# Last layers: seven layer-1 blocks of unit 1 ahead of all layer 2, and the output weights' low parts and sums on VectorE

## The chip, the cores and the metric

One core of a Trainium2 chip runs the whole program. The metric is device time in microseconds (us), the median of several runs. The kernel before takes 671.37 us (three runs, 671.11 to 671.58).

Engines are named as in the profile: PE is TensorE, PEld its weight loads, DVE is VectorE, ACT is ScalarE, POOL is GpSimd, SP is SyncE, which issues most of the DMAs. Each runs its own instructions in program order and waits on semaphores for the others.

## The reference

Attention with pooled keys, then a mixture of eight experts of which each token uses one, then a last pair of dense layers in which the change lies:

```python
x = moe(attention(q, k, v))             # 2304 tokens x 512; tokens without a place in an expert are zero
h = x @ w_in                            # 512 x 2048, float64 weights
g = s * np.maximum(h, 0) ** 2 + b
out = (g @ w_out).astype(np.float32)    # 2048 x 512, float64 weights
```

`b` adds the same row to every token, `b` times the column sums of `w_out`.

## The kernel before

Every float32 product is made of three fp32r products (high x high, high x low, low x high), so each operand is split into a high part, a copy to fp32r, and a low part, the difference. The float64 weights come as pairs of int32 words and are first made into float32 by four steps on DVE per 128x512 piece (`Weights64.step`, L858, L861, L863, L867; here A, B, C, D) and an absolute value on ACT (L860) into one buffer `c_u`. At step B of a piece the piece before it is split: high part on ACT (L1371), low part on POOL (L1372).

The last layers (`last_layers`) work on units of 256 tokens. A unit has 16 blocks of 128 rows of the middle dimension. For one block layer 1 takes 12 matmuls into a PSUM bank (`layer1_y`, L1019); `square` makes relu on ACT (L1386) and its product with the bank on DVE (L1387) in one of four SBUF tiles `rt`; `parts` splits that into `gh` (ACT, L1392) and `gl` (POOL, L1393). Layer 2 takes six matmuls a block (L1398) into two banks that are kept for the unit, from `gh`, `gl` and the split piece `wo` of `w_out`.

`pair` does units 0 and 1 together while `w_out` is loaded (16 DMAs of 512 KB, L1433) and converted; 32 more DVE additions (`add`, L1419 and L1421) sum all high and low parts. The order is written out by hand: layer 1 of unit 0 (16 blocks, banks of all eight), layer 2 of its blocks 0 to 7, layer 1 of unit 1's blocks 0 to 7 (four banks, `ph`), layer 2 of these, layer 2 of unit 0's blocks 8 to 15, layer 1 of unit 1's blocks 8 to 15, their layer 2. Between these, `spare` puts one or two conversion steps into DVE's queue for each block. Unit 2 starts behind it; after its second block `rows` multiplies the sums by a matrix of ones (L1426).

Far ahead of this, in block 1 of the experts (`block(1)` in `main`), DVE also works through `tab`, a list of small steps that make a table of the remaining work: three steps at each of f = 3 to 7 of its layer 2, and three at each block of its layer 1.

Of the kernel before, what the change touches and what calls it, by code (L numbers as in the profile page):

```python
# [869 lines left out]


class Experts:
# [160 lines left out]
    def main(self, left, one, ps):  # L1033


        nc, tc, yt = self.nc, self.tc, self.yt
# [98 lines left out]
        def block(u, v=self.v):  # L1135
# [40 lines left out]
            for f in range(KF):  # L1176
# [4 lines left out]
                tab(u == 1, 3)  # L1181
# [164 lines left out]
def last_layers(nc, tc, c, a, pool, x, ps, out):  # L1346
# [15 lines left out]
    sums = {}  # L1362
    slots = raw[2:4]
# [10 lines left out]
    cv = Weights64(nc, KF2, lambda i: wo[i], split_out, lambda i: cf[i % 2], cu)  # L1374
    done = [0]

    def conv(n):
        for _ in range(n):
            if done[0] < cv.total:
                cv.step(done[0])  # L1380
                done[0] += 1

    def square(f, p, n):
# [3 lines left out]
        nc.vector.scalar_tensor_tensor(out=r, in0=p, scalar=0.0, in1=r, op0=ALU.max, op1=ALU.mult)  # L1387

    def parts(f, n=CU, at=None):

        at = f if at is None else at
        nc.scalar.copy(gh[:, at, :n], rt[f % 4][:, :n])  # L1392
        nc.gpsimd.tensor_sub(gl[:, at, :n], rt[f % 4][:, :n], gh[:, at, :n])  # L1393

    def layer2(p, j, f, c=slice(0, DM), at=None):
        at = f if at is None else at
        for i, (l, z) in enumerate(((gh, 0), (gh, 1), (gl, 0))):
            nc.tensor.matmul(p[:, c], lhsT=l[:, at, j * P:j * P + P], rhs=wo[f][:, z, c], start=f == 0 and i == 0, stop=f == KF2 - 1 and i == 2)  # L1398
# [17 lines left out]
    def add(i):  # L1416

        if i == 0:
            nc.vector.tensor_add(sums["acc"], wo[0][:, 0], wo[0][:, 1])  # L1419
        elif 1 < i < 2 * KF2:  # L1420
            nc.vector.tensor_add(sums["acc"], sums["acc"], wo[i // 2][:, i % 2])  # L1421

    def rows(p):
        acc, drop = sums["acc"], sums["drop"]

# [4 lines left out]
    def pair():  # L1430

        for i in range(KF2):
            nc.sync.dma_start(out=wo[i].rearrange("p c two -> p (c two)"), in_=wout[:, i])  # L1433
# [5 lines left out]
        adds = iter(range(2 * KF2))

        def spare(n):
            for _ in range(n):
                if done[0] < cv.total:
                    conv(1)
                    continue
                if "acc" not in sums:
                    nc.vector.memset(onesf, 1.0)
                    sums["acc"] = pool.tile([P, DM], F32, name="c_f0")
                    slots.append(pool.tile([P, DM], F32, name="c_f1"))
                    sums["drop"] = pool.tile([P, DM], F32, name="c_u0")  # L1450
                add(next(adds, 2 * KF2))
# [152 lines left out]
```

## Time and profile before

| | |
|---|---|
| median of three runs | 671.37 us |
| the profiled execution | 671.41 us, its span 669.4 us |
| PE busy | 598.1 us, 89% of the span |
| DVE busy | 390.7 us, 58% |
| POOL busy | 281.7 us, 42% |
| ACT busy | 254.5 us, 38% |
| mean granted PE clock | 0.942 of full speed |

The shares are means over a span whose stages have different limits. `pair` runs from 339 to 450 us; the table says nothing about that stage by itself. A row of the timeline is one instruction, or several alike: its start, how long, its engine, line and operation, and in brackets the idle time of its engine ahead of it and what ended that.

### The profile page before, as it was taken

The page shows a single profiled execution, that of the slowest core. Times are in us where ns is not written, and L with a number is a line of the kernel's source. Part 1 is how long each engine was busy: PE and PEld are TensorE (multiplying, and loading weights), DVE is VectorE, ACT ScalarE, POOL GpSimd, SP SyncE. Part 2 cuts the span into 40 slices and gives each one's busy share as a digit, 9 for nine tenths or more (in the row PEclk, how much of TensorE's full clock was granted, in tenths as well). Part 3 has the DMA queues.
Part 4 walks back from the last instruction along what each step waited for, and adds up shares of the span by engine and source line. Part 5 has one row for each costly group of instructions (what it writes and reads, how often), then busy time and mean ns, then how long its engine had stood idle before and what let it go on. Part 6 is the DMA issues. An engine that isn't in the chain of part 4 may idle for free.

```text
span 669.4 us, 11104 instructions
## 1 busy us (share of the span) xinstructions
PE 598.1 (89%) x4005; PEld 553.2 (83%) x4005; DVE 390.7 (58%) x876; ACT 254.5 (38%) x619; POOL 281.7 (42%) x306
## 2 busy tenths in 40 slices
PE   5797979689889979997997689899999999999896
PEld 5686878589889979996897488788889899898785
DVE  4599798976968958661629759993412022031140
ACT  1354455435535635533336334224314124043030
POOL 5458234414133506013219746453815326044291
PEclk8698799889979989997999789999999999999989
DMA  8988576536818994755549200017210100100000
GB/s 164 201 175 183 120 199 208 197 107 213 298 65 273 288 321 135 253 182 162 163 146 385 72 1 1 1 31 272 78 62 1 48 17 2 48 17 2 35 1 19
DMA packets 67949, 86.10 MB, mean 129 GB/s; under 512 B 24713, under 2 KB 40073, under 8 KB 67856
## 3 DMA queue, kind: packets, MB, share of 16 engines
q1 hardware_dynamic: 57696, 71.34, 35.2%
q10 hardware_dynamic: 7712, 6.84, 3.4%
q0 software_dynamic: 2448, 6.82, 3.2%
q8 instruction: 42, 0.69, 0.4%
q14 instruction: 51, 0.42, 0.2%
HBM read 68.09 MB, written 17.58 MB: 128 GB/s over the span
## 4 chain that ended last, share of the span: by engine, by line
PE 51%; DVE 24%; issue 9%; DMA 7%; POOL 5%; ACT 2%; SPq 1%; POOLq 0%; ACTq 0%; another core or an unknown queue 0%; DVEq 0%
PE bank L1398 10%; PE bank L1092 9%; PE bank L1019 7%; PE tq L1019 4%; PE misc L1019 4%; DVE c_f L1421 4%; DMA vraw<-in_v_dram 4%; PE bank L946 3%; PE bank L1227 2%; DVE c_f L863 2%; PE misc L946 2%; PE tq L946 2%; DVE c_f L861 1%; DMA wg<-in_moe_w_gate_dram 1%; DVE c_f L858 1%
## 5 line engine op out<-in xcount | busy, mean ns | idle before, releaser
L1398 PE MATMUL bank<-wo,gh 128*128 128x512 f32 (+1 forms) x448 | 134.6, 383 | 13.9 <-POOL wo L1372 9.6
L1393 POOL TENSOR_TENSOR gl<-rt,gh 128x256 fp32r<-128x256 f32 (+1 forms) x112 | 89.1, 804 | 78.4 <-ACT gh L1392 54.0
L1398 PEld LDWEIGHTS bank<-wo,gh 128*128 128x128 f32 x448 | 83.1, 192 | 32.5 <-POOL wo L1372 11.3
L1398 PE MATMUL bank<-wo,gl 128*128 128x512 f32 (+1 forms) x224 | 85.3, 381 | 0.0
L1092 PE MATMUL bank<-hs,w2h 128*128 128x288 f32 (+1 forms) x308 | 70.6, 318 | 4.9 <-issue 4.5
L915 POOL TENSOR_TENSOR w1l<-kraw,w1h 128x512 fp32r<-128x512 f32 x24 | 33.8, 1422 | 66.3 <-ACT w1h L911 66.2
L1405 DVE SCALAR_TENSOR_TENSOR raw<-bank,sb,c_u 128x512 f32<-128x512 f32 (+1 forms) x14 | 9.9, 710 | 85.5 <-PE bank L1398 85.5
L1092 PEld LDWEIGHTS bank<-hs,w2h 128*128 128x128 f32 x308 | 52.6, 199 | 5.8 <-issue 5.3
L1386 ACT ACTIVATE rt<-tq 128x256 f32<-128x256 f32 (+1 forms) x26 | 9.6, 368 | 116.9 <-PE tq L1019 93.4
L1398 PEld LDWEIGHTS bank<-wo,gl 128*128 128x128 f32 x224 | 43.1, 192 | 7.7
L1387 DVE SCALAR_TENSOR_TENSOR rt<-bank,rt 128x256 f32<-128x256 f32 (+1 forms) x60 | 24.2, 403 | 39.3 <-ACT rt L1386 39.3
L1092 PE MATMUL bank<-hs,w2l 128*128 128x288 f32 (+1 forms) x148 | 45.9, 310 | 0.0
L1392 ACT CAST gh<-rt 128x256 fp32r<-128x256 f32 (+1 forms) x112 | 43.2, 385 | 3.2 <-DVE rt L1387 3.0
L923 POOL DMA_INDIRECT xg<-xd,u_idx x23 | 26.0, 1130 | 34.9 <-DVE r L279 17.7
L1406 POOL DMA_INDIRECT out_dram<-raw,it x12 | 12.0, 999 | 62.6 <-DVE raw L1405 62.1
L1386 ACT ACTIVATE rt<-bank 128x256 f32<-128x256 f32 (+1 forms) x60 | 22.3, 371 | 40.8 <-PE bank L1019 27.0
L1372 POOL TENSOR_TENSOR wo<-c_f,wo 128x512 fp32r<-128x512 f32 x16 | 24.8, 1554 | 23.0 <-ACT wo L1371 23.0
L219 PE MATMUL sc<-kbd,qT 128*128 128x144 f32 (+1 forms) x152 | 26.3, 323 | 4.5 <-DVE rmine L369 2.8
L1092 PEld LDWEIGHTS bank<-hs,w2l 128*128 128x128 f32 x148 | 29.4, 198 | 0.0
L264 PE MATMUL o<-vx,eT 128*128 128x146 f32 (+1 forms) x144 | 24.3, 317 | 5.4 <-DVE lt L283 4.7
L219 PEld LDWEIGHTS sc<-kbd,qT 128*128 128x128 f32 (+1 forms) x152 | 22.7, 207 | 6.4 <-issue 3.5
L919 DVE TENSOR_TENSOR w2l<-vraw,w2h 128x512 fp32r<-128x512 f32 x39 | 26.8, 687 | 1.0 <-ACT w2h L918 0.5
(465 smaller groups left out, 1692.6 us busy)
## 6 DMA issues: line engine op xcount, KB each, us to landing
kraw<-in_moe_w_dram SPq DMA_DIRECT2D x14, 1024.0 KB
vraw<-in_moe_w_dram SPq DMA_DIRECT2D x14, 1024.0 KB
wo<-in_moe_w_out_dram SPq DMA_DIRECT2D x16, 512.0 KB
c_raw<-in_moe_w_in_dram ACTq DMA_DIRECT2D x13, 512.0 KB
kraw<-in_k_dram SPq DMA_DIRECT2D x8, 576.0 KB
out_dram<-c_u SPq DMA_DIRECT2D x1, 4608.0 KB
q<-in_q_dram SPq DMA_DIRECT2D x16, 256.0 KB
xd<-xr SPq DMA_DIRECT2D x16, 256.0 KB
```

The source lines that it names most:

```text
L219: nc.tensor.matmul(sc[:n, p // 2, p % 2 * 144:p % 2 * 144 + 144], lhsT=q[:, p, :n], rhs=kbd[b % 2][:, p], start=True, stop=True)
L915: eng.tensor_sub(self.w1l[:, i], self.w1(i), self.w1h[:, i])
L919: eng.tensor_sub(self.w2l[i], self.w2r[:, i], self.w2h[i])
L923: self.nc.gpsimd.indirect_dma_start(out=dst, out_offset=None, in_=self.xd[:have], in_offset=bass.IndirectOffsetOnAxis(ap=idx[:n], axis=0), ...
L946: self.nc.tensor.matmul(p, lhsT=l[:, f, k], rhs=r[k], start=n == 0, stop=n == 3 * KD - 1)
L1019: self.nc.tensor.matmul(p[:, :CU], lhsT=l[:, k], rhs=r[:, k], start=n == 0, stop=n == 3 * KD - 1)
L1092: nc.tensor.matmul(py[d][:, :v.n], lhsT=l[f][:, d * P:d * P + P], rhs=r[f], start=f == 0 and i == 0, stop=f == KF - 1 and i == 2)
L1386: nc.scalar.activation(r, p, AF.Relu)
L1392: nc.scalar.copy(gh[:, at, :n], rt[f % 4][:, :n])
L1393: nc.gpsimd.tensor_sub(gl[:, at, :n], rt[f % 4][:, :n], gh[:, at, :n])
L1398: nc.tensor.matmul(p[:, c], lhsT=l[:, at, j * P:j * P + P], rhs=wo[f][:, z, c], start=f == 0 and i == 0, stop=f == KF2 - 1 and i == 2)
L1421: nc.vector.tensor_add(sums["acc"], sums["acc"], wo[i // 2][:, i % 2])
```

## The change

In `pair`, the first seven blocks (`HEAD`) of unit 1's layer 1 now stand right behind unit 0's layer 1, ahead of all layer 2; then come layer 2 of blocks 0 to 6 of both units, layer 1 of unit 1's blocks 7 to 15, and layer 2 of blocks 7 to 15 of unit 0 and of unit 1. Parts of unit 1 lie in three spare tiles, in the places of the last two pieces of `w_out` (loaded later, behind layer 2 of the first seven blocks) and in places of `gh` and `gl` that unit 0 has left.

The low parts of `w_out` move from POOL to DVE (L1375), the split of unit 1's tokens too (`split_y`, at blocks 10 to 13 of unit 0). The 32 additions of high and low parts become 15 additions of whole pieces, in step C of the next piece, and a copy on ACT (L1380 and L1382). In every third block (f % 3 == 2) the product stays in the PSUM bank; ACT and DVE split it from there. In `block(1)` of the experts `tab` makes four steps at f = 2 to 7 of layer 2 and two at each block of layer 1.

```diff
 class Weights64:
-        self.pieces, self.total = pieces, 4 * pieces + 2
+        self.pieces, self.total = pieces, 4 * pieces + (3 if late else 2)
...
+        if s == 2 and self.late and 0 < i <= self.pieces:
+            self.late(i - 1, self.f(i - 1).bitcast(F32))
...
-                tab(u == 1 and f > 2 or u == 2, 3 if u == 1 or f < KF - 1 else 99)
+                tab(u == 1 and f > 1 or u == 2, 4 if u == 1 else 3 if f < KF - 1 else 99)
...
-                tab(u == 1, 3)
+                tab(u == 1, 2)
...
     def split_out(i, f):
         w = wo[i] = pool.tile([P, 2, DM], F32R, name=f"wo{i}")
         nc.scalar.copy(w[:, 0], f)
-        nc.gpsimd.tensor_sub(w[:, 1], f, w[:, 0])
+        nc.vector.tensor_sub(w[:, 1], f, w[:, 0])
+
+    def add(i, f):
+        if i:
+            nc.vector.tensor_add(raw[3], raw[3], f)
+        else:
+            nc.scalar.copy(raw[3], f)
...
-    def square(f, p, n):
+    def square(f, p, n, inside=False):
         r = rt[f % 4][:, :n]
         nc.scalar.activation(r, p, AF.Relu)
-        nc.vector.scalar_tensor_tensor(out=r, in0=p, scalar=0.0, in1=r, op0=ALU.max, op1=ALU.mult)
+        nc.vector.scalar_tensor_tensor(out=p if inside else r, in0=p, scalar=0.0, in1=r, op0=ALU.max, op1=ALU.mult)
...
+    def parts(f, n=CU, u=0, p=None):
+        h, l = place(f, u)
+        r = rt[f % 4][:, :n] if p is None else p
+        nc.scalar.copy(h[:, :n], r)
+        (nc.gpsimd if p is None else nc.vector).tensor_sub(l[:, :n], r, h[:, :n])
...
         def first(u, f0, f1, banks):
             for n, f in enumerate(range(f0, f1)):
                 p = banks[f % len(banks)][:, :CU]
                 if u or f >= EARLY:
                     x.layer1_y(u, p, *win[f])
-                square(f, p, CU)
-                spare(2 if u == 0 and n % 4 == 3 else 1)
+                inside = f % 3 == 2
+                square(f, p, CU, inside)
+                conv(1, steps_of_first)
+                if u == 0 and 10 <= f < 10 + KD:
+                    x.split_y(1, f - 10, nc.vector)
...
-        first(0, 0, KF2, ps)
-        for k in range(KD):
-            x.split_y(1, k, nc.gpsimd)
-        second(0, 0, KF, 2)
-        first(1, 0, KF, ph)
-        x.load_y(2)
-        second(1, 0, KF, 2)
-        second(0, KF, KF2, 2)
-        first(1, KF, KF2, ph)
-        tokens(2)
-        second(1, KF, KF2, 2)
-        for i in adds:
-            add(i)
+        first(0, 0, KF2, ps)
+        first(1, 0, HEAD, ph)
+        x.load_y(2)
+        second(0, 0, HEAD, steps_of_first)
+        second(1, 0, HEAD, steps_of_first)
+        for i in range(KF2 - 2, KF2):
+            wo[i] = pool.tile([P, DM, 2], I32, name=f"wo{i}")
+            load_out(i)
+        first(1, HEAD, KF2, ph)
+        conv(all_steps, steps_of_first)
+        second(0, HEAD, KF2, all_steps)
+        tokens(2)
+        second(1, HEAD, KF2, all_steps)
+        conv(all_steps)
```

`second` puts two steps (`conv(2, ...)`) behind each block's matmuls, as before.

On PE, the place behind unit 0's last block of layer 1 (`bank_1888`) read before:

```order
L1019 MATMUL bank_1888<-yhl,w2l 128x256
L1398 MATMUL bank_1885<-wo_16673,gh 128x512 x2
L1398 MATMUL bank_1885<-wo_16673,gl 128x512
L1398 MATMUL bank_1886<-wo_16673,gh 128x512 x2
L1398 MATMUL bank_1886<-wo_16673,gl 128x512
```

and reads now, with `y1h` and `y1l` the split tokens of unit 1:

```order
L1022 MATMUL bank_1888<-yhl,w2l 128x256
L1022 MATMUL tq<-y1h,w1h 128x256
L1022 MATMUL tq<-y1l,w1h 128x256
L1022 MATMUL tq<-y1h,w1l 128x256
L1022 MATMUL tq<-y1h,w1h 128x256
```

The first matmul that needs a piece of `w_out` stands 84 matmuls (seven blocks) later.

On DVE, one piece among the layer-2 blocks was four steps before (`c_f` the piece being made, two buffers in turn):

```order
L867 SCALAR_TENSOR_TENSOR c_f_16596<-c_u_16598,c_f_16596 128x512
L858 TENSOR_SCALAR c_f_16597<-wo_16609 128x512
L861 SCALAR_TENSOR_TENSOR c_f_16597<-wo_16609,c_f_16597 128x512
L863 SCALAR_TENSOR_TENSOR c_f_16597<-wo_16609,c_f_16597 128x512
L867 SCALAR_TENSOR_TENSOR c_f_16597<-c_u_16598,c_f_16597 128x512
```

and is six instructions now, with the low part of the piece before (`wo_17057`) behind B and its addition to the sum (`raw_1904`) behind C:

```order
L868 SCALAR_TENSOR_TENSOR c_f_16596<-c_u_16598,c_f_16596 128x512
L859 TENSOR_SCALAR c_f_16597<-wo_16609 128x512
L862 SCALAR_TENSOR_TENSOR c_f_16597<-wo_16609,c_f_16597 128x512
L1375 TENSOR_TENSOR wo_17057<-c_f_16596,wo_17057 128x512
L864 SCALAR_TENSOR_TENSOR c_f_16597<-wo_16609,c_f_16597 128x512
L1380 TENSOR_TENSOR raw_1904<-raw_1904,c_f_16596 128x512
L868 SCALAR_TENSOR_TENSOR c_f_16597<-c_u_16598,c_f_16597 128x512
```

The additions had stood in a row behind the last piece.

On DVE in unit 0's layer 1, blocks 9 to 12 now hold squares (L1400), steps, a low part in PSUM (L1415) and the split of unit 1's tokens (L1015):

```order
L862 SCALAR_TENSOR_TENSOR c_f_16596<-wo_16614,c_f_16596 128x512
L1375 TENSOR_TENSOR wo_16766<-c_f_16597,wo_16766 128x512
L1415 TENSOR_TENSOR gl<-tq,gh 128x256
L1400 SCALAR_TENSOR_TENSOR rt_1911<-bank_1883,rt_1911 128x256
L864 SCALAR_TENSOR_TENSOR c_f_16596<-wo_16614,c_f_16596 128x512
L1380 TENSOR_TENSOR raw_1904<-raw_1904,c_f_16597 128x512
L1015 TENSOR_TENSOR y1l<-yr,y1h 128x256
L1400 SCALAR_TENSOR_TENSOR bank_1884<-bank_1884,rt_1912 128x256
L868 SCALAR_TENSOR_TENSOR c_f_16596<-c_u_16598,c_f_16596 128x512
L1015 TENSOR_TENSOR y1l<-yr,y1h 128x256
```

Before, this place held squares and steps alone, and the tokens of unit 1 were split on POOL.

## Rows read from the trace of the kernel before

**Rows 1.** Stages of `pair`: window, length, busy per engine, clock, DMA share, GB/s.
```profile
339.16:362.18 23.02, 23.02 (x195) 22.82 (x193) 14.26 (x24) 10.36 (x30) 12.14 (x11) 1.00 0.74 266
362.18:390.37 28.19, 16.45 (x49) 11.36 (x49) 23.01 (x29) 11.69 (x27) 21.06 (x18) 0.81 0.35 131
414.06:427.77 13.71, 11.52 (x49) 8.86 (x48) 13.09 (x17) 3.62 (x7) 6.71 (x4) 1.00 0.00 0
438.82:449.74 10.92, 10.92 (x51) 9.02 (x49) 10.61 (x12) 2.31 (x7) 6.82 (x7) 1.00 0.16 48
```

**Rows 2.** Timeline of PE: waits in layer 2, and at `rows`.
```profile
378.84 0.80 PE L1398 MATMUL bank<-wo,gh 128*128 128x512 f32 x1 [5.03 <-POOL wo L1372]
...
453.90 1.12 PE L1426 MATMUL tq<-c_f,onesf 128*128 128x512 f32 x2 [1.17 <-DVE rt L1387]
```

**Rows 3.** Timeline of DVE at unit 0's layer 1, first piece and last square.
```profile
348.29 0.43 DVE L858 TENSOR_SCALAR c_f<-wo 128x512 int32<-128x512 int32 x1 [6.53 <-DMA wo<-in_moe_w_out_dram]
348.63 0.41 DVE L1387 SCALAR_TENSOR_TENSOR rt<-misc,rt 128x256 f32<-128x256 f32 x1
348.97 0.68 DVE L861 SCALAR_TENSOR_TENSOR c_f<-wo,c_f 128x512 int32<-128x512 int32 x1
...
369.11 0.43 DVE L1387 SCALAR_TENSOR_TENSOR rt<-bank,rt 128x256 f32<-128x256 f32 x1 [0.65 <-ACT rt L1386]
```

**Rows 4.** Timeline of DVE: one piece, POOL idle until its last D.
```profile
381.86 0.69 DVE L867 SCALAR_TENSOR_TENSOR c_f<-c_u,c_f 128x512 f32<-128x512 f32 x1
382.47 0.42 DVE L858 TENSOR_SCALAR c_f<-wo 128x512 int32<-128x512 int32 x1
382.92 0.69 DVE L861 SCALAR_TENSOR_TENSOR c_f<-wo,c_f 128x512 int32<-128x512 int32 x1
383.65 0.69 DVE L863 SCALAR_TENSOR_TENSOR c_f<-wo,c_f 128x512 int32<-128x512 int32 x1
384.44 1.56 DVE L867 SCALAR_TENSOR_TENSOR c_f<-c_u,c_f 128x512 f32<-128x512 f32 x1
```

**Rows 5.** Timeline of ACT and POOL at the same piece.
```profile
382.58 0.69 ACT L860 ACTIVATE c_u<-wo 128x512 f32<-128x512 f32 x1 [5.09 <-DVE c_f L867]
383.17 0.61 ACT L1371 CAST wo<-c_f 128x512 fp32r<-128x512 f32 x1
383.85 1.60 POOL L1372 TENSOR_TENSOR wo<-c_f,wo 128x512 fp32r<-128x512 f32 x1 [3.84 <-ACT wo L1371]
```

**Rows 6.** Timeline: DVE's additions beside POOL's `gl`.
```profile
434.46 0.84 POOL L1393 TENSOR_TENSOR gl<-rt,gh 128x256 fp32r<-128x256 f32 x1 [0.31 <-ACT gh L1392]
...
434.96 0.89 DVE L1421 TENSOR_TENSOR c_f<-c_f,wo 128x512 f32<-128x512 f32 x1
435.77 0.41 DVE L1387 SCALAR_TENSOR_TENSOR rt<-tq,rt 128x256 f32<-128x256 f32 x1
...
438.72 1.10 DVE L1421 TENSOR_TENSOR c_f<-c_f,wo 128x512 f32<-128x512 f32 x1
439.74 0.41 DVE L1387 SCALAR_TENSOR_TENSOR rt<-bank,rt 128x256 f32<-128x256 f32 x1
```

**Rows 7.** Instructions of L1012 on DVE: count, duration min/median/max in ns, first and last start.
```profile
L1012 DVE TENSOR_TENSOR yhl<-yr,yhl x4: 417/417/426, 336.7 to 337.7; 128x256 fp32r<-128x256 f32 x4
```

**Rows 8.** The chain that ended last: PE's first blocks behind a wait.
```profile
390.57 2.56 PE tq L1019 x12
...
393.13 1.65 PE misc L1019 x12
```

**Rows 9.** Experts' block 1 and 2: timeline of DVE and PE, and a window.
```profile
159.48 0.46 DVE L939 TENSOR_TENSOR xs<-tq,xs 128x288 fp32r<-128x288 f32 x1 [0.66 <-ACT xs L938]
...
185.33 0.45 DVE L949 SCALAR_TENSOR_TENSOR hs<-tq,hs 128x288 fp32r<-128x288 f32 x1
...
185.84 0.74 PE L937 MATMUL tq<-ident,xg 96*128 96x96 f32 x3 [3.36 <-DVE hs L949]
...
186.00:192.00 6.00, 6.00 (x27) 5.99 (x28) 3.00 (x10) 1.83 (x4) 1.74 (x1) 0.50 0.37 132
```

More of the change, by code (lines that the diff above doesn't have):

```diff
@@ L563 @@
 EARLY = 4
+HEAD = 7
 MORE = 64
@@ L1036, in main @@
         nc, tc, yt = self.nc, self.tc, self.yt
+        self.w = left
         w2h, w2l = self.w2h, self.w2l
@@ L1361, in last_layers @@
     ph, po = ps[0:4], ps[4:8]
-    sums = {}
-    slots = raw[2:4]
+    sums, more, spare, slots = {}, [], [], []
     v8 = lambda z: z.rearrange("p (k c) -> p k c", k=KD)
@@ L1375, in last_layers, with conv @@
+    steps = [(z, n) for z in cvs for n in range(z.total)]
     done = [0]
-    def conv(n):
+    def conv(n, end=len(steps)):
         for _ in range(n):
-            if done[0] < cv.total:
-                cv.step(done[0])
+            if done[0] < end:
+                z, i = steps[done[0]]
+                z.step(i)
                 done[0] += 1
-    def square(f, p, n):
+    def square(f, p, n, inside=False):
         r = rt[f % 4][:, :n]
         nc.scalar.activation(r, p, AF.Relu)
-        nc.vector.scalar_tensor_tensor(out=r, in0=p, scalar=0.0, in1=r, op0=ALU.max, op1=ALU.mult)
@@ L1389, in parts @@
[L1389 to L1398, printed above, removed]
+        nc.vector.scalar_tensor_tensor(out=p if inside else r, in0=p, scalar=0.0, in1=r, op0=ALU.max, op1=ALU.mult)
@@ L1400, in store, with layer2 @@
+    def layer2(p, j, f, c=slice(0, DM), u=0):
+        h, l = place(f, u)
+        for i, (g, z) in enumerate(((h, 0), (h, 1), (l, 0))):
+            nc.tensor.matmul(p[:, c], lhsT=g[:, j * P:j * P + P], rhs=wo[f][:, z, c], start=f == 0 and i == 0, stop=f == KF2 - 1 and i == 2)
     def store(u, j, p):
@@ L1414, in tokens, with load_out @@
                 x.split_y(u, k, nc.gpsimd)
[L1416 to L1421, printed above, removed]
     def rows(p):
-        acc, drop = sums["acc"], sums["drop"]
-        nc.tensor.matmul(p, lhsT=onesf, rhs=acc, start=True, stop=True)
+        drop = sums["drop"]
+        nc.tensor.matmul(p, lhsT=onesf, rhs=raw[3], start=True, stop=True)
         nc.vector.tensor_scalar(out=drop, in0=p, scalar1=sb[:, 1:2], scalar2=None, op0=ALU.mult)
         nc.sync.dma_start(out=out.rearrange("(n p) d -> p n d", p=P), in_=drop.unsqueeze(1).to_broadcast([P, T // P, DM]))
+    def load_out(i):
+        nc.sync.dma_start(out=wo[i].rearrange("p c two -> p (c two)"), in_=wout[:, i])
     def pair():
-        for i in range(KF2):
-            nc.sync.dma_start(out=wo[i].rearrange("p c two -> p (c two)"), in_=wout[:, i])
+        for i in range(KF2 - 2):
+            load_out(i)
             if i == 5:
@@ L1437, in pair @@
                     nc.sync.dma_start(out=sb[:, j:j + 1], in_=a[n].unsqueeze(0).to_broadcast([P, 1]))
+        more.extend(pool.tile([P, 2, 2, CU], F32R, name=f"wo{i}") for i in range(KF2 - 2, KF2))
+        spare.extend(x.w.tile([P, 2, CU], F32R, name=f"raw{i}") for i in range(3))
         held = []
[L1439 to L1451, printed above, removed]
+        nc.gpsimd.memset(onesf, 1.0)
         def first(u, f0, f1, banks):
```

26 lines of the change are left out of this document (19 added, 7 removed).

## The prediction

> **What bounds the kernel now.** I read the stages first, by windows, then PE's waits there, then the engine that these lead to. Layer 1 of unit 0 runs at full clock, 16 blocks in 23.02 us or 1.44 us each. Eight blocks of layer 2 at full clock take 10.92 us, 1.365 each, but the first eight take 28.19: PE is busy 16.45 of it, at a granted clock of 0.81, and unit 0's second eight take 13.71 [rows 1]. Against 10.92 that is 20 us over. PE's longest wait there is 5.03 us for a low part of `w_out` from POOL, and at `rows` it waits 1.17 us more for a square on DVE, which stands behind the last additions [rows 2]. Behind POOL stands DVE: it gets its first piece of `w_out` when the DMA lands at 348.29 [rows 3] and is busy 10.61 of 10.92 us still at the last eight blocks [rows 1]. So the stage is a queue of DVE work from 348.29 on, stretched by POOL; PE can gain at most what it waits for that queue.
>
> **The free pace of DVE.** With POOL idle, D to the next A is 0.61 us, A to B 0.45, B to C 0.73 [rows 4]; 0.61 is a 128x512 instruction followed by one that doesn't need its result. A followed by a square, or a square, takes 0.34 [rows 3]. A 128x256 subtraction from SBUF is 0.417 long [rows 7], as long as a square, which reads PSUM (0.41 long, 0.34 to the next [rows 3]); for it and for the one from PSUM, which no row shows, I take 0.36, between 0.34 and 0.42 if nothing overlaps: 0.7 us for all 11 below. Each of POOL's `gl` beside DVE makes an addition's start-to-next 0.81 to 1.02 [rows 6], so 0.20 to 0.41 more than 0.61; I take 0.31.
>
> **Stretch I: from 348.29 to the end of the seven blocks put ahead.** DVE has 22 squares x 0.34 = 7.5; 23 steps, of them 6 A x 0.34 = 2.0 and 17 B, C, D x 0.61 = 10.4; 5 low parts and 4 additions x 0.61 = 5.5; 7 low parts from PSUM and 4 of unit 1's tokens x 0.36 = 4.0. Sum 29.3. POOL keeps 15 `gl` beside them x 0.31 = 4.7. One wait for ACT of about the 0.65 seen at 369.11 [rows 3], taken as 0.5. DVE ends at 348.3 + 34.5 = 382.8. Check on the same engine before: from 348.29 to 369.11 [rows 3] stood 14 squares, 5 A and 13 other steps, 14.4 at the free pace, in 20.8 us, with POOL always busy. PE starts unit 1's block 0 piecemeal, as its tokens are split in blocks 10 to 13 of DVE's queue, and idles for some 6 us after 362; that is covered, since it waits for DVE later anyway.
>
> **Stretch II: layer 2 of the first seven blocks of both units.** DVE has 28 steps, seven pieces, without squares and with POOL idle. A piece's low part waits for ACT: D starts at 381.86, the absolute value behind it at 382.58, the copy at 383.17, and the subtraction that waited for the copy (on POOL then) started at 383.85, 1.99 after D [rows 4, 5]. On DVE alone it could start after 0.61 + 0.45 + 0.61 = 1.67, so 0.32 is a wait that the change adds; C, the addition and D stand behind it. Then three times 0.61 to the next D: 3.82 a piece, 26.7 in all (24.5 if the wait goes, at 3.5; with C to D at the 0.79 of a step that needs the one before it [rows 4] in three places, 4.4 a piece and 30.6). DVE ends at 409.5. PE meanwhile: piece 6's low part is done at 382.8 + 1.99 + 0.69 + 3.82 = 389.3, block 6 of unit 0 at 390.7, seven blocks of unit 1 at 400.2, four layer-1 blocks into the four banks at 406.0. Then it waits until DVE's square of block 7, 0.41 behind 409.5: about 410.0, a wait of 4 us.
>
> **Stretch III: the rest.** Behind a wait like that PE's first layer-1 blocks took 2.56 and 1.65 us at half clock [rows 8]. Block 11 ends at 412.6. Block 12 needs block 8's low part from PSUM: DVE has three squares, D, A, B, a low part and that one in front, 3.55 + 0.31 for a `gl`, so 413.4; it ends at 415.0, and three more x 1.44 at 419.4. Then 18 blocks of layer 2 x 1.365 = 24.6: unit 2 starts at 444.0. The last two pieces' loads follow 400 and their low parts end near 429, ahead of need; the sums too, so the wait of 1.17 at `rows` goes. Before, unit 2 started at 449.74 [rows 1]. Gain 5.7 + 1.2 = 6.9 us.
>
> **Experts' block 1.** The same steps of `tab` stand earlier. Before, PE waited 3.36 us for a read of a bank that DVE reached at 185.33, and then 6.0 us ran at a granted clock of 0.50, the lower of the two levels [rows 9]: 3.0 us lost. Now four steps more stand ahead of that read, about 0.7, but a first lot fills the 0.66 in which DVE waited at 159.48 [rows 9]. So that read stays where it was; the reads of blocks 0 to 5 come later, PE waits for these in pieces, and less at the end. Bounds: 3.3 gained (no drop of the clock) to 1.0 lost; I take 2.0 gained, nearer the row at half clock.
>
> **Sum.** 671.41, the profiled execution's own time (its span 669.4 and 2.0 around it; 0.04 above the median) less 6.9 and 2.0: 662.5, and I forecast 662.4 against the median. PE runs without a stage-sized wait from unit 2's start nearly to the end, so the shift stays.
>
> **Rivals.**
>
> *GpSimd's lock.* A `gl` of 0.84 us cost DVE 0.20 to 0.41 [rows 6]. If it costs its whole length in the thicker queue, where two of three DVE instructions read SBUF twice, stretch I grows by 15 x 0.53 = 8.0 and III by 0.5: 671.0, no change. For it: the D at 384.44 took 1.56 instead of 0.69 us beside POOL's `wo` [rows 4, 5]. Against it: the check above, where POOL was never idle, gave 20.8 for 14.4. The Trainium skill has this rule, on its page "SBUF — State Buffer", "Who interferes with whom": a Vector instruction with two SBUF inputs and a GpSimd instruction that reads SBUF block each other for the whole instruction. The additions' 0.20 to 0.41 show a part of it only.
>
> *The stretch isn't POOL's doing: slower.* If DVE's ratio of 20.8 to 14.4 comes from the mixture of squares and steps itself (waits for ACT among them), it holds in stretch I and II alike, though POOL has less to do: 29.3 + 24.5 (seven pieces at 3.5 free) times 1.45 is 78.0 where I have 61.2, and unit 2 starts 16.8 later: 679.2. It decides from 70.2 us on; between, each microsecond of the queue is one of the gain. For it: DVE's queue is longer than before at this point by low parts that were POOL's, and PE stands in order behind it. Against it: the free pieces at 381.86 to 383.65 [rows 4].
>
> *PE bounds it.* With no cost of `gl` and no wait for ACT, DVE needs 29.3 + 24.5, ends at 402.1, and PE waits only 2 us there; unit 2 starts near 436.0. With 3.3 from block 1: 653.2.
>
> **How the numbers follow.** Forecast 0.62; lock 0.13; slower 0.11; PE-bound 0.14. The forecast's own range is 658 to 668: 0.5 us on each of the seven pieces, 3 on stretch I, 2 on block 1. The range for 8 in 10 is 655 to 672; it leaves out the slower rival and the far end of the third. A measurement tells 0.2%, 1.3 us, from no change. Faster: 0.61 of the forecast's, 0.06 of the lock's and the third's 0.14, 0.81; within 0.2%: 0.08; slower 0.11.
>
> **What would show it.** Stretch I: DVE's seventh square of unit 1 near 381. Stretch II: D to D 3.8 us, with a wait for ACT of 0.3 ahead of each L1375. Stretch III: PE waits some 4 us near 406, then at L1022 half clock, and unit 2's layer 1 starts 5 to 6 us earlier against the experts' end than before. `rows`: no wait. Block 1: no window of 6 us at 0.50 behind 186. I am wrong if D to D is above 5.1 ((70.2 - 34.5) / 7), if PE doesn't wait for the squares behind the fourth block, or if the wait for banks at 186 is as long as before with the same clock.

## The result, and the profile after

The changed kernel took 665.51 us (median of 4 runs, 664.22 to 665.70) against 671.48 before (4 runs, 671.11 to 673.56): a ratio of 0.9901, 95% interval 0.9877 to 0.9924, which is 6.6 us less (the medians differ by 6.0). The forecast was 662.4, a ratio of 0.9866. The profiled execution took 665.48 and has a span of 663.8.

First, where the 5.6 us of span came from: PE's timeline at the places where stages begin and where it waits. Columns as in [rows 2].

```profile
157.17 0.51 PE L1096 MATMUL bank<-hs,w2h 128*128 128x288 f32 x2 [0.43 <-DVE u_lists L428]
...
215.65 0.43 PE L1096 MATMUL bank<-hs,w2h 128*128 128x288 f32 x2
...
410.05 0.38 PE L1022 MATMUL bank<-y1h,w2h 128*128 128x256 f32 x1 [3.81 <-DVE rt L1400]
...
413.52 0.58 PE L1022 MATMUL tq<-y1h,w2h 128*128 128x256 f32 x1 [1.24 <-DVE gl L1415]
...
445.62 0.41 PE L1022 MATMUL tq<-yhl,w1h 128*128 128x256 f32 x2
...
448.46 1.02 PE L1441 MATMUL tq<-raw,onesf 128*128 128x512 f32 x2
```

And the first two of these rows, block 1's and block 3's first product, in the kernel before:

```profile
153.17 0.51 PE L1092 MATMUL bank<-hs,w2h 128*128 128x288 f32 x2 [0.43 <-DVE u_lists L428]
...
214.36 0.43 PE L1092 MATMUL bank<-hs,w2h 128*128 128x288 f32 x2
```

The experts' block 1 starts 4.0 us *later* than before, behind instructions that are the same in both kernels. From there to block 3's first product (L1096; 215.65, 214.36 before) it is 58.48 for 61.19, 2.7 us gained. The first piece of `w_out` lands 0.96 later in the span (349.25 for 348.29). From the landing to `rows` it is 99.21 for 105.61 [rows 2, 3]: 6.4 us gained, `rows`' wait of 1.17 among them. Behind `rows` both take 210.7 to their last instruction. So the two edits gained 9.1 in this pair of profiles, and 4.0 went ahead of both.

The stages of `pair`, by windows (columns as in [rows 1]): layer 1 of unit 0; up to where layer 1 of unit 1 stood before; from block 8 of unit 1 into its block 12; the rest.

```profile
340.66:363.52 22.86, 22.86 (x196) 22.86 (x194) 14.69 (x30) 12.52 (x36) 7.66 (x9) 1.00 0.72 265
363.52:390.37 26.85, 22.04 (x127) 19.23 (x126) 25.85 (x49) 13.20 (x33) 7.95 (x8) 0.94 0.28 101
401.83:415.18 13.35, 8.30 (x57) 7.80 (x56) 12.79 (x25) 6.31 (x15) 2.48 (x3) 0.84 0.09 36
415.18:445.62 30.44, 30.44 (x150) 26.13 (x150) 12.86 (x22) 7.21 (x18) 6.81 (x8) 0.96 0.07 18
```

PE is busy 22.04 of 26.85 where it was busy 16.45 of 28.19 [rows 1], and the rest holds no wait. DVE is still full, 25.85 of 26.85 and 12.79 of 13.35. POOL has little to do.

DVE at the landing, at the end of stretch I (the sixth D, at 382.99), over one piece, and at the square of block 7:

```profile
349.25 0.43 DVE L859 TENSOR_SCALAR c_f<-wo 128x512 int32<-128x512 int32 x1 [5.99 <-DMA wo<-in_moe_w_out_dram]
...
382.99 0.68 DVE L868 SCALAR_TENSOR_TENSOR c_f<-c_u,c_f 128x512 f32<-128x512 f32 x1
383.59 0.41 DVE L859 TENSOR_SCALAR c_f<-wo 128x512 int32<-128x512 int32 x1
384.04 0.69 DVE L862 SCALAR_TENSOR_TENSOR c_f<-wo,c_f 128x512 int32<-128x512 int32 x1
384.96 0.69 DVE L1375 TENSOR_TENSOR wo<-c_f,wo 128x512 fp32r<-128x512 f32 x1 [0.23 <-ACT wo L1374]
385.57 0.68 DVE L864 SCALAR_TENSOR_TENSOR c_f<-wo,c_f 128x512 int32<-128x512 int32 x1
386.17 0.69 DVE L1380 TENSOR_TENSOR raw<-raw,c_f 128x512 f32<-128x512 f32 x1
386.77 0.68 DVE L868 SCALAR_TENSOR_TENSOR c_f<-c_u,c_f 128x512 f32<-128x512 f32 x1
...
409.58 0.42 DVE L1400 SCALAR_TENSOR_TENSOR rt<-bank,rt 128x256 f32<-128x256 f32 x1
```

A piece takes 3.78 from D to D, with the wait for ACT that the change adds (0.23) ahead of L1375.

At the end of the experts' block 1 PE waits in four pieces, and the 6 us behind the last of them run at full clock, where [rows 9] had one wait of 3.36 and a granted clock of 0.50 behind it:

```profile
178.99 0.54 PE L949 MATMUL bank<-xs,w1h 128*128 128x288 f32 x2 [0.81 <-DVE hs L952]
...
181.35 0.40 PE L949 MATMUL bank<-xs,w1h 128*128 128x288 f32 x1 [0.50 <-DVE hs L952]
...
185.39 0.54 PE L949 MATMUL misc<-xs,w1h 128*128 128x288 f32 x2 [0.47 <-DVE hs L952]
...
189.96 0.47 PE L940 MATMUL tq<-ident,xg 96*128 96x96 f32 x3 [1.13 <-DVE hs L952]
```

```profile
190.00:196.00 6.00, 6.00 (x49) 6.00 (x50) 3.52 (x8) 2.76 (x6) 2.12 (x2) 1.00 0.52 186
```

The four pieces still add up to 2.91 us. Most of the 2.7 gained there is therefore the clock, and only some 0.5 is waiting.

### The profile page after: what moved, and what is told of

The parts are those of the page before. It is cut to its first block, busy times and chain, and to the rows that moved or that the text cites. A ratio compares the mean times of both kernels' runs of the same rounds, so it can differ in the third digit from the quotient of the medians.

```text
span 663.8 us, 11041 instructions
## 1 busy us (share of the span) xinstructions
PE 596.7 (90%) x4005; PEld 554.0 (83%) x4005; DVE 377.2 (57%) x889; ACT 254.1 (38%) x620; POOL 241.9 (36%) x277
## 5 line engine op out<-in xcount | busy, mean ns | idle before, releaser
L1420 PE MATMUL bank<-wo,gh 128*128 128x512 f32 (+1 forms) x412 | 119.2, 374 | 1.2 <-ACT wo L1374 1.0
L1415 POOL TENSOR_TENSOR gl<-rt,gh 128x256 fp32r<-128x256 f32 (+1 forms) x96 | 72.6, 761 | 110.3 <-ACT gh L1414 59.2
L1420 PEld LDWEIGHTS bank<-wo,gh 128*128 128x128 f32 x412 | 74.9, 188 | 15.0 <-ACT wo L1374 1.4
L1420 PE MATMUL bank<-wo,gl 128*128 128x512 f32 (+1 forms) x206 | 76.8, 373 | 0.0
L1096 PE MATMUL bank<-hs,w2h 128*128 128x288 f32 (+1 forms) x308 | 69.1, 313 | 6.1 <-issue 5.7
L918 POOL TENSOR_TENSOR w1l<-kraw,w1h 128x512 fp32r<-128x512 f32 x24 | 34.0, 1432 | 64.8 <-ACT w1h L914 64.4
L1096 PEld LDWEIGHTS bank<-hs,w2h 128*128 128x128 f32 x308 | 51.3, 194 | 7.1 <-issue 6.5
L1096 PE MATMUL bank<-hs,w2l 128*128 128x288 f32 (+1 forms) x148 | 45.1, 305 | 0.0
L1420 PEld LDWEIGHTS bank<-wo,gl 128*128 128x128 f32 x206 | 38.8, 188 | 6.8
L1400 DVE SCALAR_TENSOR_TENSOR rt<-bank,rt 128x256 f32<-128x256 f32 (+1 forms) x53 | 21.3, 401 | 38.5 <-ACT rt L1399 38.2
L1414 ACT CAST gh<-rt 128x256 fp32r<-128x256 f32 (+1 forms) x96 | 36.6, 381 | 6.5 <-DVE rt L1400 6.5
L1400 DVE SCALAR_TENSOR_TENSOR rt<-tq,rt 128x256 f32<-128x256 f32 (+1 forms) x24 | 9.6, 400 | 36.4 <-ACT rt L1399 36.4
L1096 PEld LDWEIGHTS bank<-hs,w2l 128*128 128x128 f32 x148 | 28.7, 194 | 0.0
L264 PEld LDWEIGHTS o<-vx,eT 128*128 128x128 f32 (+1 forms) x144 | 20.2, 194 | 9.1 <-issue 7.1
L949 PE MATMUL bank<-xs,w1h 128*128 128x288 f32 (+1 forms) x120 | 26.1, 302 | 1.3 <-DVE hs L952 1.3
## 6 DMA issues: line engine op xcount, KB each, us to landing
wo<-in_moe_w_out_dram SPq DMA_DIRECT2D x16, 512.0 KB
c_raw<-in_moe_w_in_dram ACTq DMA_DIRECT2D x13, 512.0 KB
```

Of the source, the lines that this page charges most:

```text
L264: nc.tensor.matmul(o[:n, p // 2, p % 2 * 2 * VW:p % 2 * 2 * VW + 2 * VW], lhsT=et[:, p, :n], rhs=two_cols(vx[g][:, 2 * p:2 * p + 2]), star ...
L918: eng.tensor_sub(self.w1l[:, i], self.w1(i), self.w1h[:, i])
L949: self.nc.tensor.matmul(p, lhsT=l[:, f, k], rhs=r[k], start=n == 0, stop=n == 3 * KD - 1)
L1096: nc.tensor.matmul(py[d][:, :v.n], lhsT=l[f][:, d * P:d * P + P], rhs=r[f], start=f == 0 and i == 0, stop=f == KF - 1 and i == 2)
L1400: nc.vector.scalar_tensor_tensor(out=p if inside else r, in0=p, scalar=0.0, in1=r, op0=ALU.max, op1=ALU.mult)
L1414: nc.scalar.copy(h[:, :n], r)
```

## The experiments

The theory to be tested: each edit does what the prediction's steps say, and the 4.0 us ahead of them have nothing to do with the change. Beside the experiments the kernel before ran 44 times on three chips and took 667.34 to 676.16, so one time carries a chance of several us. Four lengths, one execution each, are therefore read from each trace as well: when block 1 starts; from there to block 3's first product ("blocks"); and, counted from the landing of `w_out`'s first piece, the square of block 7 (unit 1) and the start of unit 2.

```
kernel       block 1   blocks   square 7   unit 2   ratio to before (95%)
before       153.17    61.19      -        101.4    
before_2     157.58    59.90      -        102.2    (one time, 673.70)
before_3     155.50    61.01      -         99.9    (one time, 673.35)
tab_only     154.01    58.49      -        100.2    0.9968 (0.9943 to 0.9993)
pair_only    155.65    59.92    60.3        94.4    0.9892 (0.9854 to 0.9929)
after        157.17    58.48    60.3        96.4    0.9901 (0.9877 to 0.9924)
again        157.29    58.48    60.2        94.5    0.9902 (0.9867 to 0.9937)
low_on_pool  155.55    58.60    63.4        98.1    0.9857 (0.9819 to 0.9895)
no_inside    157.40    58.51    61.3        94.9    0.9835 (0.9801 to 0.9869)
order_only   152.87    58.48    64.5        98.7    0.9926 (0.9886 to 0.9965)
hold         159.56    58.47    53.2        95.7    0.9860 (0.9835 to 0.9885)
both         154.03    58.47    53.3        88.6    0.9783 (0.9757 to 0.9809)
all          157.20    58.46    51.5        86.9    0.9758 (0.9733 to 0.9783)
all_short    147.72    58.59    51.4        86.8    0.9646 (0.9600 to 0.9691)
```

**The two edits apart.** pair_only is the changed kernel with the old `tab` calls, tab_only the kernel before with the new ones:

```diff
-tab(u == 1 and f > 2 or u == 2, 3 if u == 1 or f < KF - 1 else 99)
+tab(u == 1 and f > 1 or u == 2, 4 if u == 1 else 3 if f < KF - 1 else 99)
...
-tab(u == 1, 3)
+tab(u == 1, 2)
```

> The change's last layers with the experts' tab steps back at their old places. The stages ahead of the experts' block 1 run the same instructions in every kernel here, and yet the changed kernel's block 1 started 4.0 us later than before (157.17 against 153.17). My theory: block 1's edit gained 3.5 us there (the later start of 4.0 us at 153 is down to 0.45 us at 217) and that is all it does. So here PE waits about 3.4 us in one piece near 190 and then runs at the lower clock for some 6 us, and the time is 665.5 + 3.5 = 669.0 if the 4.0 us come with the new last layers (another program behind the same early instructions). Rival: the 4.0 us come with the tab edit; then block 1 starts near 153 and the time is 665.0. Third: the early stages come out by chance in each program, anywhere from 1 us earlier to 5 us later than before; then the time less the start of block 1 is what carries the terms: 512.0 here against 508.3 after and 518.2 before.

> The kernel before with the tab edit alone. My theory: block 1 gains 3.5 us: no single wait of 3.4 us near 186, no 6 us at the lower clock behind it; time 671.4 - 3.5 = 667.9 with block 1 starting near 153. Rival, that the tab edit brings the late start: block 1 starts near 157, time 671.9. Third, that the start comes out by chance: the time less the start of block 1 is 514.7 wherever it starts (518.2 before).

With the old calls "blocks" is 59.90 to 61.19 in four profiles, with the new ones 58.46 to 58.60 in ten, whatever the last layers: 2.0 us on the means (60.5 and 58.5). pair_only shows the wait in one piece again:

```profile
188.34 0.74 PE L940 MATMUL tq<-ident,xg 96*128 96x96 f32 x3 [3.35 <-DVE hs L952]
```

```profile
188.50:194.50 6.00, 6.00 (x38) 6.00 (x39) 3.00 (x10) 2.21 (x6) 1.74 (x1) 0.73 0.42 127
```

The 6 us behind it run at 0.73 here and at 0.50 in the kernel before [rows 9]: 1.4 us of clock, where the two lengths differ by 1.3. In tab_only the longest such wait is 1.1. The ratios agree: 0.9968 is 2.2 us, 0.9892 is 7.3. They don't add up to the 6.6 us of both edits together; with intervals 3 to 5 us wide the times can't say why. pair_only came out at 665.71, not 669.0, and tab_only at 669.62, not 667.9: the expectation had read block 1's worth (3.5) and the 4.0 us from a single pair of profiles. Block 1 started at 155.65 and 154.01, neither 157 nor 153, as only the third reading (chance) allows; but the time less that start is 508.2 and 515.7 in the profiled executions (663.85 and 669.67), where that reading had 512.0 and 514.7: what follows varies by some us too.

**Where the 4.0 us come from.** again, before_2 and before_3 are the two kernels unaltered.

> The changed kernel unaltered, once more. The program before took 667.75 to 675.45 us in 17 runs beside the first experiments, and four profiles of kernels that run the same instructions up to the experts' block 1 started it anywhere from 153.2 to 157.4. My theory: the 4.0 us by which block 1 started later than before in the first profile were chance; the edits are worth 6.7 (last layers) and 2.1 (block 1) of the time before, a ratio of 0.987 to the kernel before on this chip. In the profile, counted from the landing of the first piece of w_out: the fifth multiplication that ends a piece (L868) ends stretch I at 33.7, the square of block 7 stands at 60.3, unit 2 starts at 94 to 97. Rival: the early stages are slower in this program for good: block 1 starts at 157 again and the ratio is 0.990 or more.

> The kernel before, unaltered, for its trace. My theory: the start of the experts' block 1 comes out by chance, by whether a short VectorE instruction with two inputs in SBUF (L149, L337) starts while a GpSimd addition of 1.3 to 2.4 us (L145, L147) runs; then it ends when that ends. Two paths were seen: L149 at 0.29 and the first L337 at 0.20 us, block 1 at 153.2 to 155.7; or both at 1.2 to 1.3, block 1 at 155.6 to 159.6. Both paths were seen with the new last layers, the second never yet in the two profiles with the old. By my theory this profile may show either. Rival: the second path belongs to programs with the new last layers; then here the first, block 1 at 153 to 154.

> As before_2, a third profile of the kernel before. By chance: either path, block 1 between 153 and 160. Rival: the first path again, 153 to 154.

again came out as its rival said, on both counts: block 1 at 157.29 and a ratio of 0.9902. But the kernel before starts block 1 at 153.17, 157.58 and 155.50 in three executions, against the rival that it always starts early: a late start isn't the new program's alone. A place where the ways part is near 44 us, in attention. DVE and then POOL there, in the kernel before as first profiled:

```profile
45.20 0.41 DVE L147 TENSOR_TENSOR vraw<-vraw 128x256 f32<-128x256 f32 x1
45.65 0.29 DVE L149 TENSOR_TENSOR vp<-vraw 128x128 f32<-128x128 f32 x1
...
45.93 2.36 POOL L145 TENSOR_TENSOR kraw<-kraw 72x1024 f32<-72x1024 f32 x1 [2.12 <-DMA kraw<-in_k_dram]
```

In the changed kernel:

```profile
44.09 2.35 POOL L145 TENSOR_TENSOR kraw<-kraw 72x1024 f32<-72x1024 f32 x1 [2.04 <-DVE lt L283]
46.52 1.32 POOL L147 TENSOR_TENSOR kraw<-kraw 72x512 f32<-72x512 f32 x1
...
44.17 2.56 DVE L147 TENSOR_TENSOR vraw<-vraw 128x256 f32<-128x256 f32 x1
46.76 1.23 DVE L149 TENSOR_TENSOR vp<-vraw 128x128 f32<-128x128 f32 x1
```

And in before_2, the late one of the old kernel:

```profile
44.80 2.32 DVE L149 TENSOR_TENSOR vp<-vraw 128x128 f32<-128x128 f32 x1
...
44.38 2.59 POOL L145 TENSOR_TENSOR kraw<-kraw 72x1024 f32<-72x1024 f32 x1 [1.41 <-DMA kraw<-in_k_dram]
```

POOL starts when what it waits for is there, a load in two of the three. If that is after DVE's two short instructions, they take 0.41 and 0.29; if POOL is 0.08 us ahead, as in the changed kernel, the first takes 2.56 and ends just behind POOL's (46.73, POOL 46.44), and the next waits for POOL's next. Later places of the same kind (L337, 0.20 or 1.30) follow. Over the 13 profiles (all_short apart) the two ways stay apart: seven with that L149 at 1.23 to 2.32 and a long first L337 (0.78 to 1.31) reach the last L337 at 142.7 to 145.2 us, the other six at 140.4 to 141.9.

That is part of the 4.0 alone. From the last L337 (141.08 before, 143.54 after, 2.5 later) to block 1 the two executions differ by another 1.5, with PE at another granted clock. The kernel before, then the changed one:

```profile
141.10:153.17 12.07, 11.02 (x88) 10.55 (x89) 9.68 (x54) 5.76 (x14) 0.23 (x1) 1.00 0.43 138
```

```profile
143.50:157.17 13.67, 12.55 (x89) 12.09 (x89) 10.07 (x55) 5.79 (x14) 0.23 (x1) 0.88 0.48 165
```

In all 13 this stretch takes 12.1 us at a granted clock of 1.00 (three profiles), 13.4 to 13.6 at 0.87 to 0.88 (five) or 14.3 to 14.7 at 0.78 to 0.80 (five), for old and new programs alike and on either way. So the 4.0 us are some 2.5 that go with the way taken near 44 us and some 1.5 of clock. All this is settled ahead of any instruction that the change touches.

What the runs don't settle is whether the new program falls into the late way more often. Of the four profiles with the old last layers one goes it, of the nine with the new ones six, and in these six L147 is held (1.66 to 2.56 us), which none of the old four shows. Block 1 started at 155.1 in the mean of the four, at 156.3 in the nine, and the ratio of again is 2.4 us short of the forecast's, at the edge of its interval.

**Where low parts are made.** low_on_pool puts `w_out`'s low parts on GpSimd again, no_inside all low parts of blocks, order_only both:

```diff
-        nc.vector.tensor_sub(w[:, 1], f, w[:, 0])
+        nc.gpsimd.tensor_sub(w[:, 1], f, w[:, 0])
...
-                inside = f % 3 == 2
+                inside = False
```

> The changed kernel with the low parts of w_out on GpSimd again, all else kept. My theory: on VectorE a low part costs 0.61 and a wait of 0.24 for ScalarE; on GpSimd it takes 1.6 and stretches one VectorE instruction by 0.87 (1.56 for 0.69 before), so a piece of stretch II stays at about 3.9 us (3.80 after), and PE gets piece 6 0.9 us later: 666.5, range 665 to 668. Rival, the lock for the whole instruction: each of 13 low parts ahead of the square of block 7 costs VectorE 1.6 - 0.85 more, 9.8 us: 675. Other rival, VectorE gains all 0.85 back in each piece: 13 x 0.85 = 11 us less queue, of which PE can use the 8 us that it loses near 410: 657.5.

> The changed kernel with every block's low part on GpSimd from SBUF, none on VectorE from PSUM. My theory: ahead of stretch II VectorE is spared 7 x 0.36 = 2.5 us and pays for 7 more instructions of GpSimd at 0.26 to 0.31 each, 2.0: no change, 665.0, range 664 to 666.5. Rival, the lock for the whole instruction (0.84 each): 7 x 0.84 - 2.5 = 3.4 us later: 668.9. Rival, GpSimd costs VectorE nothing in the mean: 663.0.

> The changed kernel's order, with both of its edits to low parts undone: GpSimd makes every low part of w_out and of each block, as before. Counted from the landing of the first piece of w_out: low parts of w_out on GpSimd alone moved the square of block 7 from 60.3 to 63.4, and all the blocks' low parts on GpSimd alone to 61.3. My theory: the two add up, square of block 7 at 64.4, unit 2 at 98 to 100 (94.4 to 96.4 in the changed kernel, 100.2 to 101.4 before, and before has a wait of 1.2 behind it too); the order alone is then worth some 3 us, less than half of the last layers' gain, and the ratio to before is 0.993 with block 1's 2 us. Rival: GpSimd now has the most to do (22 + 7 instructions), and its queue sets the end of stretch I: unit 2 at 101 or later, no gain from the order. Other rival: the order does it all, and moving work between the two engines nothing: unit 2 at 96 or less.

Square 7 answers, since it came at 60.2 to 60.3 in all three profiles of the changed last layers: 63.4, 61.3 and 64.5, expected 60.3 + 3.1 + 1.0 = 64.4 for the last. Expected for the first two were a delay of 0.9 us and none. Unit 2 comes at 98.7 in order_only, against 99.9 to 102.2 before with 1.2 more at `rows`. So the order, with the shorter sums and the tokens' split on VectorE that order_only keeps, is worth some 3.5 us and the low parts on VectorE some 3.5, of 7.2 in all; the two halves rest on one execution of order_only. By `rows` low_on_pool alone loses 3.0 (100.9 for 97.9) and no_inside nothing (97.7): the split in PSUM brings no gain that a run shows.

The times don't resolve the halves, and went another way than expected: low_on_pool took 663.26 (expected 665 to 668) and no_inside 661.93 (664 to 666.5). no_inside has the best ratio of the three and order_only (0.9926) the worst, with intervals some 5 us wide; that of no_inside ends at 0.9869, below the 0.9877 at which that of the changed kernel begins. Which stage makes no_inside faster isn't shown.

The last addition of one piece and the first rows of the next in low_on_pool, DVE and then POOL:

```profile
388.02 0.69 DVE L864 SCALAR_TENSOR_TENSOR c_f<-wo,c_f 128x512 int32<-128x512 int32 x1
388.63 1.75 DVE L1380 TENSOR_TENSOR raw<-raw,c_f 128x512 f32<-128x512 f32 x1
390.30 0.68 DVE L868 SCALAR_TENSOR_TENSOR c_f<-c_u,c_f 128x512 f32<-128x512 f32 x1
...
388.20 1.63 POOL L1375 TENSOR_TENSOR wo<-c_f,wo 128x512 fp32r<-128x512 f32 x1 [2.44 <-ACT wo L1374]
```

The instruction that was under way when POOL started keeps its 0.69; the one that starts 0.43 into POOL's 1.63 lasts until 0.55 behind POOL's end. So the price is about what is left of POOL's instruction when the next VectorE instruction comes: 1.06, with 1.20 left, and a piece takes 4.06 to 4.10 for 3.80. A `gl` in the changed kernel shows the same, POOL first:

```profile
354.52 0.92 POOL L1415 TENSOR_TENSOR gl<-rt,gh 128x256 fp32r<-128x256 f32 x1 [1.01 <-ACT gh L1414]
...
354.77 1.22 DVE L1375 TENSOR_TENSOR wo<-c_f,wo 128x512 fp32r<-128x512 f32 x1
```

It ends at 355.99, 0.55 behind POOL. An instruction that reads PSUM isn't held. Beside the next `gl` a square keeps its 0.41, and that `gl` takes 0.74:

```profile
356.84 0.74 POOL L1415 TENSOR_TENSOR gl<-rt,gh 128x256 fp32r<-128x256 f32 x1 [1.40 <-ACT gh L1414]
...
357.18 0.41 DVE L1400 SCALAR_TENSOR_TENSOR rt<-bank,rt 128x256 f32<-128x256 f32 x1
```

The Trainium skill's page "SBUF — State Buffer", "Who interferes with whom", says that a Vector instruction with two SBUF inputs and a GpSimd instruction that reads SBUF block each other for the whole instruction. The rows at 388.63 and 354.77 agree for a VectorE instruction that comes second.

**PE's wait for the square of block 7.** hold leaves 7 of stretch II's 28 steps for later (one step a block of unit 1 in place of two); both does so (three steps a block) and takes each block of layer 2 for unit 0 and unit 1 before the next block (`tokens(2)` then stands behind block 11); all adds an earlier split of unit 1's tokens, and has ScalarE make a piece's high part (early) ahead of the next piece's absolute value:

```diff
 hold
-        second(1, 0, HEAD, steps_of_first)
+        second(1, 0, HEAD, steps_of_first, 1)
 both
-        second(0, 0, HEAD, steps_of_first)
-        second(1, 0, HEAD, steps_of_first)
+        both(0, HEAD, steps_of_first, 3)
...
-        second(0, HEAD, KF2, all_steps)
-        second(1, HEAD, KF2, all_steps)
+        both(HEAD, KF2, all_steps, 4)
 all
-                if u == 0 and 10 <= f < 10 + KD:
+                if u == 0 and 8 <= f < 8 + KD:
...
+        if s == 1 and self.early and 0 < i <= self.pieces:
+            self.early(i - 1, self.f(i - 1).bitcast(F32))
```

> The changed kernel with 7 of the 28 conversion steps of stretch II left for later, so that VectorE's square of block 7 isn't queued behind them. My theory: the square of block 7 comes at 60.3 - 7 x 0.95 = 53.7 after the landing of w_out's first piece, PE's wait of 3.8 us there and the half clock behind it go, but pieces 13 to 15 end later and unit 0's blocks of layer 2 wait for them: unit 2 starts at 95 to 98 after the landing (94.4 and 96.4 in two profiles without the edit): no gain, 0 to +1.5 us. Rival: VectorE's later pieces are ahead of need anyway, PE keeps what it saves, some 7 us: unit 2 at 88.

> As hold, and in both parts of layer 2 each block is taken for unit 0 and unit 1 before the next block, so that each piece of w_out is needed up to 9.5 us later. My theory: the waits of PE at 39.5 (1.0 us) and at 60.8 (3.8 us) go, with 1.5 to 3 us of half clock behind the second; pieces 13 to 15 are ready in time: unit 2 starts at 87 to 89 after the landing of the first piece, 6 to 8 us earlier than in the changed kernel. Rival: VectorE's queue bounds the whole of these layers, and the wait moves to the last pieces: unit 2 at 94 or later.

> As both, and unit 1's tokens are split two blocks earlier (blocks 8 to 11 of unit 0 in place of 10 to 13), and ScalarE makes a piece's high part ahead of the next piece's absolute value. My theory: the wait of 0.24 for ScalarE ahead of each piece's subtraction goes (3.55 from piece to piece in stretch II for 3.80), PE's waits for the split tokens (3.6 us near 15 to 20) shrink by 2 or more with the half clock behind them: unit 2 starts at 83 to 86. Rival: PE only comes earlier to a piece that VectorE hasn't made; then no more than both.

hold takes the wait of 3.81 away and unit 2 comes no earlier (95.7): PE now waits for a late piece of `w_out` in unit 0's blocks.

```profile
429.53 0.50 PE L1420 MATMUL bank<-wo,gh 128*128 128x512 f32 x1 [2.07 <-ACT wo L1374]
```

```profile
429.50:437.50 8.00, 7.21 (x16) 4.73 (x17) 4.33 (x6) 1.84 (x5) 3.51 (x4) 0.59 0.00 1
```

Behind that wait the granted clock is 0.59 over 8 us, so what hold saved at one place it paid at the next. both needs each piece later, and that wait goes too. Of PE's waits those for the split tokens stay (0.65, 0.39 and 2.63 between 361 and 366), and one for a block's low part, the first row here; the second is unit 2's start:

```profile
404.25 0.38 PE L1022 MATMUL tq<-y1h,w2h 128*128 128x256 f32 x1 [1.54 <-DVE gl L1415]
...
434.64 0.40 PE L1022 MATMUL tq<-yhl,w1h 128*128 128x256 f32 x2
```

Unit 2 comes at 88.6, expected 87 to 89, and the time is 657.01 (0.9783). In all a piece of stretch II takes 3.47, the free pace, without the wait for ACT, but unit 2 gains only 1.7 more (86.9, expected 83 to 86): the rival that PE only comes earlier to what VectorE hasn't made is nearer for that part. PE waits 0.65 for the split tokens where it waited 3.7, and 2.3 and 1.65 for VectorE's squares and low parts further on.

**GpSimd's long additions in attention.** all_short is all with them cut in two by heads:

```diff
         def pool_all(kv, b, h0, h1, eng):
+            if eng is nc.gpsimd and h1 - h0 > 2:
+                m = (h0 + h1) // 2
+                pool_all(kv, b, h0, m, eng)
+                pool_all(kv, b, m, h1, eng)
+                return
```

> The fastest kernel so far, all, with GpSimd's additions of three or more heads in the attention stage cut in two, so that none that stands beside VectorE's short instructions is longer than about 1.3 us (2.35 before). My theory: a VectorE instruction that meets one waits for its end, so the longest stays fall from 2.4 to 1.3 us; block 1 starts at 153 to 156 (157.2 in all) and the time is 653 to 656 (656.2). Rival: the additions cost GpSimd more in two parts than in one and the stage waits for them: block 1 at 158 or later, 657 or more.

```profile
42.37 1.27 POOL L145 TENSOR_TENSOR kraw<-kraw 72x512 f32<-72x512 f32 x1 [0.57 <-DMA kraw<-in_k_dram]
43.72 0.79 POOL L147 TENSOR_TENSOR kraw<-kraw 72x256 f32<-72x256 f32 x1
...
42.86 1.06 DVE L147 TENSOR_TENSOR vraw<-vraw 128x256 f32<-128x256 f32 x1
43.96 0.70 DVE L149 TENSOR_TENSOR vp<-vraw 128x128 f32<-128x128 f32 x1
```

The two instructions of VectorE take 1.06 and 0.70 beside POOL, for 2.56 and 1.23. Block 1 starts at 147.72 (expected 153 to 156), earlier than in any of the 13 profiles without it, and the time is 647.09 (642.95 to 649.75): 23 us less than before; less than all by 9.1 on the medians and 7.5 by the two ratios, beyond my range of 653 to 656. The lengths behind block 1 are as in all, so nearly all of the gain lies ahead of it. It is more than falling into the early way: the instruction that is the last L337 in the others stands at 134.1, 6.3 ahead of the earliest of the 13. The waits are shorter as expected, the size isn't explained: that a first half is ready earlier may be another part, and these weren't told apart.

## Why the prediction was right where it was, and what failed

**Stretch I: right.** 33.7 us from landing to the D at 382.99 (the sixth; the expectation of again counts it as the fifth), forecast 34.5; the unaltered kernel's second profile and pair_only repeat it within 0.15. PE idled 3.6 us there for the split tokens (forecast some 6), covered as said. The price of a `gl` was right in the mean and wrong as a picture. The rows above show a lock: whoever comes second waits for the other's end. It costs 0.54 where VectorE comes second (1.22 for 0.68), nothing where it is reading PSUM or under way, and some of it falls on POOL (0.92 for the 0.74 of a `gl` beside instructions that read PSUM). The rival of the lock therefore had the right mechanism and the wrong price: it charged the whole 0.84 every time, 12.6 for 15 `gl`, and by its sum unit 2 would have come 8.5 us later than the forecast's. The lengths in the traces give the mean: against 0.68 for a 128x512 instruction that meets no lock and 0.42 for the others, VectorE's instructions beside the 16 of GpSimd in stretch I are 4.0 us longer in all, 0.25 each, for my 0.31. The seven more in no_inside cost above it, 0.35 each by these lengths, or 0.5 by square 7 (1.0 later, with 2.5 of VectorE's own work spared by my count).

**Stretch II: right.** 26.6 from there to the square of block 7, forecast 26.7; 3.78 to 3.82 a piece, forecast 3.82; the added wait for ACT 0.22 to 0.26, forecast 0.32. all confirms the other bound, 3.5 without it. The slower rival needed 5.1 a piece and is out.

**PE's wait and stretch III: right in place, the size by chance.** PE waits 3.81 at 410.05 (4 forecast). Behind it the granted clock varies: a window of 7.8 us behind the wait of the changed kernel, and the same of pair_only, which runs the same code there (the lower of the two levels is 0.50):

```profile
409.80:417.60 7.80, 6.30 (x31) 6.01 (x32) 7.03 (x15) 4.03 (x11) 2.88 (x3) 0.57 0.00 0
```

```profile
410.20:418.00 7.80, 7.08 (x48) 6.79 (x49) 7.47 (x17) 5.16 (x14) 2.86 (x3) 0.78 0.00 0
```

At the two levels 0.57 is 6.7 us at half clock and 0.78 is 3.4; the forecast had two blocks, 4.2 us, at it. That is most of why unit 2 comes 96.4 and 94.4 after the landing; again gave 94.5. The forecast, 444.0 - 348.3 = 95.7, lies between. The wait at `rows` is gone, as said. Over all profiles the last layers gained 7.2 from landing to `rows` (105.1, mean of four; 97.9, mean of three), forecast 6.9.

**Experts' block 1: right.** 2.0 on the means, 2.0 forecast, with the waits in pieces and no window at 0.50. The size was partly luck: what the bound of 3.3 stood for, no drop of the clock, came true, and the mean is less because in two of the four old profiles the clock was down for a shorter time. The old kernel scatters by 1.3 there for that reason, the new one by 0.14.

**PE-bound: out as a forecast.** It put unit 2 at 87.7 after the landing; all reached 86.9, but by further edits.

**What failed: the sum.** It subtracted 8.9 from one execution of before as if all that the change leaves alone took the same time again ("so the shift stays"). The edits did gain 9.1 in the profiles, and the stages ahead of them gave back 4.0: some 2.5 with the way taken near 44 us and some 1.5 with the granted clock just ahead of block 1. That execution of before had the early way and the full clock there, and block 1 at 153.17, the earliest of the three of its program. Neither the forecast nor any rival had a term for that scatter; the range held the time only because it was wide for other reasons. Whether the 2.4 us still missing in the repeated ratio are chance or a lean of the new program stays open.

## What to carry to other kernels

Before taking a difference of two executions for an edit's worth, line up a landmark that stands ahead of the edit: here 4.0 us went where nothing had been changed. Compare the granted clock of the stretches, too. Count an engine's queue in stretches between landmarks, at the pace of free rows; the start of unit 2 came within 1.3 us so, while the new order and the moved low parts were not told apart by times with an interval of 5 us. A wait that is taken away in one place of an in-order queue (hold) is paid at the next, until the order of need is changed too (both).

## What the runs showed of the hardware

- A GpSimd addition or subtraction under way holds up a VectorE instruction with two SBUF inputs to its end: 2.56 us for one of 0.41, 1.75 for 0.69, 1.22 for 0.68; a square, which reads PSUM, keeps its 0.41 beside one. Who starts first decides, by 0.08 us in one place. Cutting the additions in two went with 7.5 to 9 us less.
- Behind a wait of 3.8 us PE's granted clock over the next 7.8 us was 0.57 in one execution and 0.78 in another of the same code; the same stretch of PE's work ahead of block 1 took 12.1 to 14.7 us in 13 executions, at granted clocks of 1.00 to 0.78.
- The same program took 667.3 to 676.2 us in 44 runs, and its block 1 started at 153.2, 155.5 and 157.6 in three profiled executions.
